# Sparse attention followed by a Mish MLP: three hand-assigned two-bank accumulators, scores in five jobs at three points of MLP2, VectorE masks placed between the normalisations

## The chip, the cores and the metric

One core of one Trainium2 chip. The metric is the device time of one execution in microseconds (us). One core alone can't be compared with another.

## The reference, cut to what matters

```python
# q, k, v: [8 batches, 8 heads, 576, 64]; heads 0-3 local, heads 4-7 strided
mask_local   = (rel >= 0) & (rel < 32)                        # rel = query - key position
mask_strided = (rel >= 0) & (key % 32 == query % 32)
attn = softmax(where(mask, q @ k.T / 8, -1e9)) @ v
x = attn.transpose(0, 2, 1, 3).reshape(4608, 512)             # 4608 tokens
h = x @ w_in                                                  # 512 -> 2048
out = (h * tanh(softplus(h))) @ w_out                         # Mish, 2048 -> 512
```

## The kernel before: the parts that matter

The 4608 tokens go through the MLP in nine blocks of 512. TensorE works on block t while the attention of a later batch is woven between its matmuls: block 0 carries batch 1, blocks 1 to 6 carry batches 2 to 7, blocks 7 and 8 carry nothing. MLP1 (x to hidden) is eight groups of eight matmuls into tiles called `psh` (in PSUM, the memory that matmuls write, eight banks of it); MLP2 (hidden to out) is sixteen steps of four matmuls into `pso`. After each MLP2 step the list below is served: `Q` computes scores and starts their exponential on ScalarE (and the mask, on the engine given), `V` multiplies masked scores by v on TensorE (the P.V below, into an output bank `po`) and normalises on VectorE, which frees that bank, `X` transposes the result into `xT`.

```python
def attn_steps(b):
    return [
        [Q("s", 0, Dv)], [], [Q("s", 1, Dv)],
        [Q("s", 2, Po), V("s", 0)],
        [Q("l", 0, Po), V("s", 1)],
        [Q("l", 1, Po), V("s", 2), V("s", 3)],
        [Q("l", 2, Po), V("s", 4)], [V("s", 5), V("s", 6)],
        [V("s", 7), V("l", 0)], [V("l", 1)], [X("s", 0), V("l", 2)],
        [X("s", 1), V("l", 3)], [X("l", 0), V("l", 4)], [V("l", 5)],
        [X("l", 1)], [],
    ]
```

So scores are entered six times a block; four of six masks are on GpSimd (`Po`), two on VectorE (`Dv`). The eight PSUM banks are split between two two-bank tiles for the MLP, one two-bank tile for scores, and two one-bank tiles for transposes and P.V outputs:

```python
ps_mm = ...tile_pool(name="psmm", bufs=2, space=PS)   # psh, pso: 2 x 2 banks
ps_s  = ...tile_pool(name="pss",  bufs=1, space=PS)   # ps: scores, 1 x 2 banks
ps_t  = ...tile_pool(name="pst",  bufs=2, space=PS)   # tr, trx, po: 2 x 1 bank
```

The prologue computes the attention of batch 0 and ends with GpSimd's own queue of work for batch 1 and 2. It is an ordered queue: what is written later waits for what is written earlier.

```python
cast_qk_loc(1, Po, Po)      # GpSimd: fp32 to bf16
cast_v(1, Po, Po)           # waits for v of batch 1 to land
load_w_out(2, 4)            # GpSimd issues: second half of w_out
load_qk_str(2)              # GpSimd issues: ks, qs of batch 2
```

The softmax here doesn't subtract the row's maximum and nothing guards it: scores larger than these inputs give would overflow.

## Time and profile before

| | before |
|---|---|
| median of 3 runs (lowest, highest) | 341.49 us (340.92, 341.49) |
| span of the profiled run | 339.5 us |
| block 0: MLP1, MLP2 | 16.45, 23.11 us |
| blocks 1 to 6: MLP1, MLP2 | 15.9 (block 4: 16.06), 19.54 us |
| blocks 7, 8: each half | 13.81 us |

The lengths of the halves are read from TensorE's timeline: from the first `psh` matmul to the first `pso`, and from there to the next first `psh`. A few matmul records are missing from a trace, so a half is now and then shown 0.2 us long and its neighbour as much short. GpSimd's queue in block 0, from the timeline (start, length, engine, line, operation, output<-input, count, and in brackets the idle time before it and what ended it):

```profile
44.98 1.89 POOL L146 CAST vs<-vs 72x2048 bf16<-72x2048 f32 x1 [15.62 <-DMA vs<-in_v_dram]
...
50.98 1.50 POOL L137 DMA_DIRECT2D w_out<-in_moe_w_out_dram  x2
...
55.41 1.29 POOL L256 TENSOR_TENSOR Ps<-Ps,consts_sb 72x576 bf16<-72x576 bf16 x1
56.64 4.83 POOL L256 TENSOR_TENSOR Pl<-Pl,consts_sb 128x768 bf16<-128x768 bf16 x3
```

The mask at 55.41 is last in the queue, behind casts and issues. TensorE stands for it before its P.V at 56.76. The cast at 44.98 could not start before v of batch 1 had landed.

### The profile page before, as it was taken

To read this page: it belongs to the slowest core of one execution; us is meant where nothing else is said; L and a number is where in the kernel's file an instruction comes from. 1 tells how busy PE (TensorE), PEld (TensorE's weight loads), DVE (VectorE), ACT (ScalarE), POOL (GpSimd) and SP (SyncE) were. 2 spreads that over 40 slices of the span, in tenths; PEclk is the share of its full clock that TensorE was granted. 3 is DMA by queue.
4 is the path that set the end of the run, shared out by engine and by line. 5 is a ranking of instruction groups with operands and counts; after the bars stand their busy time and mean duration, and the time that the engine had idled before them with its cause. 6 is when DMAs were issued, how large, how long until landed. Compare 5 with 4: busy or idle time off the path is not lost.

```text
span 339.5 us, 6425 instructions
## 1 busy us (share of the span) xinstructions
PE 313.8 (92%) x2761; PEld 171.1 (50%) x2808; DVE 114.3 (34%) x306; ACT 176.2 (52%) x194; POOL 111.0 (33%) x105
## 2 busy tenths in 40 slices
PE   2669996999999999999999999999999999999994
PEld 1554553554455545554579555544554454444441
DVE  4670345323552346134622362236323640000000
ACT  3574562556637563747464646564566537414511
POOL 4354049334681049102921094008500700000000
PEclk9999999999999999999999999999999999999999
DMA  6999958999947911595149712941010011011011
GB/s 178 217 220 205 212 95 128 215 200 284 193 110 209 188 37 64 159 198 79 63 116 202 120 62 64 229 74 60 17 51 0 2 64 62 2 62 62 0 57 68
DMA packets 49596, 39.29 MB, mean 116 GB/s; under 512 B 27168, under 2 KB 42080, under 8 KB 49568
## 3 DMA queue, kind: packets, MB, share of 16 engines
q1 hardware_dynamic: 38272, 29.88, 38.6%
q0 software_dynamic: 11152, 8.92, 16.9%
q8 instruction: 22, 0.36, 0.5%
q10 hardware_dynamic: 144, 0.08, 0.1%
q14 instruction: 6, 0.05, 0.1%
HBM read 38.34 MB, written 9.44 MB: 141 GB/s over the span
## 4 chain that ended last, share of the span: by engine, by line
PE 73%; DMA 12%; DVE 4%; POOL 3%; issue 3%; ACT 3%; SPq 1%; POOLq 0%; ACTq 0%
PE psh L368 32%; PE pso L388 28%; DMA vl<-in_v_dram 7%; DMA qs<-in_q_dram 4%; PE po L271 4%; PE tr L174 2%; PE tr L183 2%; ACT Ps L247 2%; DVE x_s L283 1%; PE ps L229 1%; DVE qTl L146 1%; PE ps L240 1%; PE trx L320 1%; PE trx L310 1%; POOL vl L146 1%
## 5 line engine op out<-in xcount | busy, mean ns | idle before, releaser
L388 PE MATMUL pso<-w_out,gT 128*128 128x512 bf16 x546 | 137.3, 379 | 1.6 <-issue 0.2
L368 PE MATMUL psh<-xT,w_in 128*128 128x512 bf16 (+1 forms) x623 | 133.1, 359 | 1.3 <-ACT gT L373 0.2
L373 ACT ACTIVATE gT<-psh 128x1024 bf16<-128x1024 f32 x72 | 73.6, 1024 | 55.7 <-PE psh L368 55.6
L368 PEld LDWEIGHTS <-w_in 128*128 128x128 bf16 x640 | 60.1, 98 | 54.6 <-issue 2.2
L388 PEld LDWEIGHTS <-gT 128*128 128x128 bf16 x576 | 49.0, 97 | 44.3
L144 ACT COPY xT<-trx 128x576 bf16<-128x576 bf16 x32 | 20.3, 639 | 44.1 <-PE trx L320 28.0
L256 POOL TENSOR_TENSOR Ps<-Ps,consts_sb 72x576 bf16<-72x576 bf16 x7 | 8.9, 1273 | 88.8 <-ACT Ps L247 88.7
L256 POOL TENSOR_TENSOR Pl<-Pl,consts_sb 128x768 bf16<-128x768 bf16 x21 | 33.8, 1638 | 1.6 <-ACT Pl L247 1.6
L395 ACT COPY osb<-pso 128x1024 f32<-128x1024 f32 x18 | 18.2, 1012 | 27.4 <-PE pso L388 27.4
L282 DVE RECIPROCAL rden<-po 72x4 f32<-72x4 f32 (+1 forms) x100 | 17.7, 177 | 35.3 <-PE po L271 35.3
L247 ACT ACTIVATE Pl<-ps 128x768 bf16<-128x768 f32 x24 | 19.5, 811 | 14.6 <-PE ps L229 14.4
L283 DVE TENSOR_TENSOR x_s<-po,rden 72x256 bf16<-72x256 f32 x56 | 23.6, 421 | 1.9
L247 ACT ACTIVATE Ps<-ps 72x864 bf16<-72x864 f32 (+1 forms) x24 | 19.1, 806 | 9.5 <-PE ps L240 9.4
L146 DVE COPY kTl<-tr 128x576 bf16<-128x576 bf16 x14 | 10.6, 758 | 30.2 <-PE tr L183 30.2
L146 POOL CAST vs<-vs 72x2048 bf16<-72x2048 f32 x7 | 13.3, 1896 | 18.3 <-DMA vs<-in_v_dram 18.3
L283 DVE TENSOR_TENSOR x_l<-po,rden 96x256 bf16<-96x256 f32 x44 | 18.5, 420 | 1.5
L256 DVE TENSOR_TENSOR Ps<-Ps,consts_sb 72x864 bf16<-72x864 bf16 (+1 forms) x17 | 10.3, 605 | 22.0 <-ACT Ps L247 22.0
L146 DVE COPY kTs<-tr 128x576 bf16<-128x576 bf16 x14 | 6.4, 458 | 30.7 <-PE tr L174 30.7
L271 PEld LDWEIGHTS <-Ps 72*128 72x128 bf16 x256 | 12.1, 102 | 8.8 <-POOL Ps L256 2.4
L271 PE MATMUL po<-vs,Ps 72*128 72x65 bf16 x224 | 14.2, 195 | 2.3 <-POOL Ps L256 2.3
L146 DVE COPY qTl<-tr 128x576 bf16<-128x576 bf16 x14 | 10.6, 756 | 14.8 <-PE tr L183 14.8
L271 PE MATMUL po<-vl,Pl 128*128 128x65 bf16 x176 | 12.9, 196 | 2.8 <-DVE rden L282 1.5
(61 smaller groups left out, 227.0 us busy)
## 6 DMA issues: line engine op xcount, KB each, us to landing
out_dram<-osb SPq DMA_DIRECT2D x18, 512.0 KB, 3.5
vl<-in_v_dram SPq DMA_DIRECT2D x7, 768.0 KB, 17.2
vs<-in_v_dram SPq DMA_DIRECT2D x8, 576.0 KB
kl<-in_k_dram SPq DMA_DIRECT2D x7, 576.0 KB
ql<-in_q_dram SPq DMA_DIRECT2D x7, 576.0 KB, 9.6
w_out<-in_moe_w_out_dram POOLq DMA_DIRECT2D x4, 512.0 KB, 12.5
ks<-in_k_dram POOLq DMA_DIRECT2D x7, 288.0 KB, 12.4
qs<-in_q_dram POOLq DMA_DIRECT2D x7, 288.0 KB, 13.8
```

What stands on the lines that cost most here:

```text
L144: nc.scalar.copy(out_, in_)
L146: eng.tensor_copy(out_, in_)
L174: nc.tensor.transpose(tr[:, PN * u:PN * u + PN], src[0:PN, h, 128 * jj:128 * jj + 128], ident[0:PN, 0:PN],)
L247: nc.scalar.activation(pt[0:n, :, 0:nw], ps[0:n, :, 0:nw], AF.Exp, scale=scale)
L256: meng.tensor_tensor(out=pm, in0=pm, in1=mk[0:n, :].unsqueeze(1).unsqueeze(1).to_broadcast([n, 2, nu, w]), op=ALU.mult,)
L271: nc.tensor.matmul(po[:, h, :], lhsT=pt[0:n, c0:c0 + 128], rhs=rhs, start=True, stop=True,)
L282: nc.vector.reciprocal(rden[0:m, :], po[0:m, :, D])
L283: nc.vector.tensor_tensor(out=dst.rearrange("p (h d) -> p h d", h=4), in0=po[0:m, :, 0:D], in1=rden[0:m, :].unsqueeze(2).to_broadcast([m, ...
L368: nc.tensor.matmul(ps[:, u, o:o + n], lhsT=w_in[:, cc, fc * 128:(fc + 1) * 128], rhs=xT[:, cc, a:a + n], start=(cc == 2), stop=(cc == 1),)
L373: nc.scalar.activation(gT[:, 2 * g:2 * g + 2, :], ps[:], AF.Mish)
L388: nc.tensor.matmul(p[:, ot % 2, :], lhsT=gT[:, fc, 128 * ot:128 * ot + 128], rhs=w_out[:, fc, :], start=(fc == 0), stop=(fc == 15),)
L395: nc.scalar.copy(osb[:], p[:])
```

## The change

Its intent: give TensorE fewer, larger visits to the scores; free the masks from GpSimd's queue and from its slower arithmetic; and let the six banks of the two-bank tiles serve whatever needs them. The diff, cut to its core:

```diff
-    ps_mm = ...tile_pool(name="psmm", bufs=2, space=PS)
-    ps_s = ...tile_pool(name="pss", bufs=1, space=PS)
+    ps_a = ...tile_pool(name="psa", bufs=1, space=PS)
+    def acc(i, name):                                  # three of these, chosen by hand
+        return ps_a.tile([128, 2, 512], F32, tag=f"acc{i}", name=name)
...                                                     # local jobs: 5, 5 and 2 units, not 4, 4, 4
-    def attn_steps(b):
+    def attn_steps(b, x, y):                           # x, y: accumulators for scores
+        if x == y:  ...                                # block 0: one accumulator, five points
         return [
+            [],
+            [Q(x, s0), Q(y, s1), M(*s0), M(*s1)],      # M: a mask, on VectorE
+            [],
+            [V("s", 0), V("s", 1)],
+            [Q(x, *sl2), Q(y, l0), V("s", 2)],         # sl2: s2 and l2 in one accumulator
+            [V("s", 3), M("s", 2), M("l", 2)],
+            [V("s", 4), M(*l0)],
+            [Q(x, l1), V("s", 5)],
+            [V("s", 6), V("l", 5), M(*l1)],
+            [V("s", 7), V("l", 0)],
+            [V("l", 1)],
+            [X("s", 0), V("l", 2)],
+            [X("s", 1), V("l", 3)],
+            [V("l", 4), X("l", 0)],
             [X("l", 1)], [],
         ]
...                                                     # mlp1 group g: accumulator g % 3
         cast_qk_loc(1, Po, Po)
-        cast_v(1, Po, Po)
-        load_w_out(2, 4)
         load_qk_str(2)                                 # now ahead of the cast of v
+        def cast_v1():                                 # called in block 0, after MLP2 step 0
+            cast(Dv, vs[1][0:PN, :, :, 0:D], vs32[0:PN])
+            Po.tensor_copy(held[:], vs[1][0:1, 3, 0, 0:4])
+            load_w_out(2, 4)
+            cast_v_loc(1, Po)
```

More of the change, by code (lines that the diff above doesn't have):

```diff
@@ L71 @@
     kTs = const.tile([128, 4 * 4 * PN + 64], BF16, name="kTs")
-    P_s = [const.tile([PN, 2, 6 * PN + 56], BF16, name=f"Ps{i}") for i in range(3)]
-    P_l = [const.tile([128, 2, 4 * WQ + 32], BF16, name=f"Pl{i}") for i in range(3)]
+    P_s = [const.tile([PN, 2, n * PN + 56], BF16, name=f"Ps{i}") for i, n in enumerate((6, 6, 4))]
+    P_l = [const.tile([128, 2, n * WQ + 32], BF16, name=f"Pl{i}") for i, n in enumerate((5, 5, 2))]
     gate = const.tile([1, 256], BF16, name="gate")
@@ L82 @@
     PS = bass.MemoryType.PSUM
-    ps_mm = ctx.enter_context(tc.tile_pool(name="psmm", bufs=2, space=PS))
-    ps_s = ctx.enter_context(tc.tile_pool(name="pss", bufs=1, space=PS))
+    ps_a = ctx.enter_context(tc.tile_pool(name="psa", bufs=1, space=PS))
     ps_t = ctx.enter_context(tc.tile_pool(name="pst", bufs=2, space=PS))
-    def tile_s(from_mm=False):
-        if from_mm:
-            return ps_mm.tile([128, 2, 512], F32, tag="mm", name="ps")
-        return ps_s.tile([128, 2, 512], F32, tag="ps", name="ps")
+    def acc(i, name):
+        return ps_a.tile([128, 2, 512], F32, tag=f"acc{i}", name=name)
     def tile_t(name):
@@ L214 @@
     S_UNITS = [(jj, h) for jj in range(4) for h in range(4)]
-    S_JOBS = [S_UNITS[0:6], S_UNITS[6:12], S_UNITS[12:16]]
-    S_AT = {u: (i, n) for i, job in enumerate(S_JOBS) for n, u in enumerate(job)}
+    L_UNITS = [(i, hp) for i in range(NW) for hp in range(2)]
+    PARTS = {
+        "s": [S_UNITS[0:6], S_UNITS[6:12], S_UNITS[12:16]],
+        "l": [L_UNITS[0:5], L_UNITS[5:10], L_UNITS[10:12]],
+    }
+    AT = {kd: {u: (i, n) for i, p in enumerate(PARTS[kd]) for n, u in enumerate(p)} for kd in "sl"}
     class Attn:
@@ L220, in __init__ @@
             self.b = b
-        def qk(self, kind, i, meng, from_mm=False):
-            ps = tile_s(from_mm)
-            if kind == "l":
-                nu, n, w, pt, mk = 4, 128, WQ, P_l[i], loc
-                for u in range(nu):
-                    hp, c0 = u // 2, WQ * (2 * i + u % 2)
-                    for e in range(2):
-                        nc.tensor.matmul(
-                            ps[:, e, WQ * u:WQ * u + WQ],
-                            lhsT=kTl[64 * e:64 * e + 64, hp, c0:c0 + 128],
-                            rhs=qTl[64 * e:64 * e + 64, hp, c0:c0 + WQ],
-                            start=True, stop=True,
-                        )
-            else:
-                nu, n, w, pt, mk = len(S_JOBS[i]), PN, PN, P_s[i], stm
-                for u, (jj, h) in enumerate(S_JOBS[i]):
-                    c0 = PN * (4 * h + jj)
-                    for e in range(2):
-                        nc.tensor.matmul(
-                            ps[:, e, PN * u:PN * u + PN],
-                            lhsT=kTs[64 * e:64 * e + 64, c0:c0 + 128],
-                            rhs=qTs[64 * e:64 * e + 64, c0:c0 + PN],
-                            start=True, stop=True,
-                        )
-            nw = nu * w
-            nc.scalar.activation(pt[0:n, :, 0:nw], ps[0:n, :, 0:nw], AF.Exp, scale=scale)
-            if meng is not None:
-                self.mask(kind, i, meng)
@@ new lines, in qk @@
+        def qk(self, parts, i_acc):
+            ps, o = acc(i_acc, "ps"), 0
+            todo = []
+            for kind, i in parts:
+                w = WQ if kind == "l" else PN
+                o0 = o
+                for x, y in PARTS[kind][i]:
+                    for e in range(2):
+                        r = slice(64 * e, 64 * e + 64)
+                        if kind == "l":
+                            lhsT, rhs = kTl[r, y, WQ * x:WQ * x + 128], qTl[r, y, WQ * x:WQ * x + WQ]
+                        else:
+                            c0 = PN * (4 * y + x)
+                            lhsT, rhs = kTs[r, c0:c0 + 128], qTs[r, c0:c0 + PN]
+                        nc.tensor.matmul(ps[:, e, o:o + w], lhsT=lhsT, rhs=rhs, start=True, stop=True)
+                    o += w
+                todo.append((kind, i, o0, o - o0))
+            for kind, i, o0, nw in todo:
+                n, pt = (128, P_l[i]) if kind == "l" else (PN, P_s[i])
+                nc.scalar.activation(pt[0:n, :, 0:nw], ps[0:n, :, o0:o0 + nw], AF.Exp, scale=scale)
@@ L251, in mask @@
         def mask(self, kind, i, meng):
-            nu, n, w, pt, mk = (
-                (4, 128, WQ, P_l[i], loc) if kind == "l" else (len(S_JOBS[i]), PN, PN, P_s[i], stm)
-            )
+            nu = len(PARTS[kind][i])
+            n, w, pt, mk = (128, WQ, P_l[i], loc) if kind == "l" else (PN, PN, P_s[i], stm)
             pm = pt[0:n, :, 0:nu * w].rearrange("p e (u c) -> p e u c", u=nu)
@@ L265, in pv_mm @@
                     n, rhs = 128, vl[self.b % 2][:, i, h, :]
-                    pt, c0 = P_l[i // 2][:, h % 2], WQ * (2 * (h // 2) + i % 2)
+                    part, u = AT["l"][i, h // 2]
+                    pt, c0 = P_l[part][:, h % 2], WQ * u
                 else:
                     n, rhs = PN, vs[self.b % 2][0:PN, h, i, :]
-                    job, u = S_AT[i // 2, h]
-                    pt, c0 = P_s[job][:, i % 2], PN * u
+                    part, u = AT["s"][i // 2, h]
+                    pt, c0 = P_s[part][:, i % 2], PN * u
                 nc.tensor.matmul(
@@ L286, in pv, with pv2 @@
             )
-        def pv2(self, kind, i, from_mm=False):
-            po = tile_s(from_mm)[:, :, 0:4 * (D + 1)].rearrange("p e (h d) -> p e h d", h=4)
+        def pv2(self, kind, i, i_acc):
+            po = acc(i_acc, "po2")[:, :, 0:4 * (D + 1)].rearrange("p e (h d) -> p e h d", h=4)
             m = WQ if kind == "l" else PN
@@ L327, in xt @@
                 )
-    def attn_steps(b):
+    def attn_steps(b, x, y):
         a = Attn(b)
-        Po, Dv = nc.gpsimd, nc.vector
-        Q = lambda kd, i, e: (lambda: a.qk(kd, i, e))
+        Q = lambda i_acc, *parts: (lambda: a.qk(parts, i_acc))
+        M = lambda kd, i: (lambda: a.mask(kd, i, nc.vector))
         V = lambda kd, i: (lambda: a.pv(kd, i))
         X = lambda kd, hf: (lambda: a.xt(kd, hf))
-        return [
-            [Q("s", 0, Dv)], [], [Q("s", 1, Dv)],
-            [Q("s", 2, Po), V("s", 0)],
-            [Q("l", 0, Po), V("s", 1)],
-            [Q("l", 1, Po), V("s", 2), V("s", 3)],
-            [Q("l", 2, Po), V("s", 4)], [V("s", 5), V("s", 6)],
-            [V("s", 7), V("l", 0)], [V("l", 1)], [X("s", 0), V("l", 2)],
-            [X("s", 1), V("l", 3)], [X("l", 0), V("l", 4)], [V("l", 5)],
+        s0, s1, sl2, l0, l1 = ("s", 0), ("s", 1), (("s", 2), ("l", 2)), ("l", 0), ("l", 1)
+        if x == y:
+            return [
+                [], [Q(x, s0)],
+                [M(*s0), Q(x, s1)],
+                [V("s", 0)],
+                [V("s", 1), M(*s1), Q(x, *sl2)],
+                [V("s", 2)],
+                [V("s", 3), M("s", 2), M("l", 2), Q(x, l0)],
+                [V("s", 4)],
+                [V("s", 5), M(*l0), Q(x, l1)],
+                [V("s", 6), V("l", 5)],
+                [V("s", 7), V("l", 0), M(*l1)],
+                [X("s", 0), V("l", 1)],
+                [X("s", 1), V("l", 2)],
+                [V("l", 3), V("l", 4)],
+                [X("l", 0), X("l", 1)], [],
+            ]
+        return [
+            [],
[12 more added lines that the diff above has]
+            [V("l", 4), X("l", 0)],
             [X("l", 1)], [],
@@ L353, in segs, with mlp1 @@
         return r
-    def mlp1(t):
+    def mlp1(t, accs):
         gT = g_pool.tile([128, 16, 512], BF16, tag="gT", name="gT")
@@ L361, in group @@
             if g not in held:
-                held[g] = ps_mm.tile([128, 2, 512], F32, tag="mm", name="psh")
+                held[g] = acc(accs[g % 3], "psh")
             ps = held[g]
@@ L378, in mlp1, with mlp2 @@
         return gT, [lambda g=g: group(g) for g in range(8)]
-    def mlp2(t, gT, fc_major=False):
+    def mlp2(t, gT, accs, fc_major=False):
         po = {}
@@ L384, in group @@
             if ot // 2 not in po:
-                po[ot // 2] = ps_mm.tile([128, 2, 512], F32, tag="mm", name="pso")
+                po[ot // 2] = acc(accs[ot // 2], "pso")
             p = po[ot // 2]
@@ L447 @@
         for i in range(3):
-            a.qk("s", i, None, i > 0)
+            a.qk([("s", i)], i)
         a.mask("s", 0, Dv)
@@ L460 @@
             t_step_loc0(kl0, kTl[:, hp, 32:32 + S], hp, Sc)
-        a.pv2("s", 0)
+        a.pv2("s", 0, 0)
         a.mask("s", 2, Dv)
-        a.pv2("s", 2, True)
+        a.pv2("s", 2, 1)
         for hp in range(2):
             t_step_loc0(ql0, qTl[:, hp, :], hp, Sc)
-        a.qk("l", 0, None, True)
-        a.pv2("s", 4)
-        a.qk("l", 1, None, True)
+        a.qk([("l", 0)], 2)
+        a.pv2("s", 4, 0)
+        a.qk([("l", 1)], 1)
         a.mask("l", 0, Dv)
-        a.pv2("s", 6)
+        a.pv2("s", 6, 0)
         cast_v_loc(0, Sc, 3, 6)
-        a.qk("l", 2, None, True)
+        a.qk([("l", 2)], 2)
         a.mask("l", 1, Dv)
@@ L477 @@
         load_v(1)
-        gT, g1 = mlp1(0)
+        accs = (2, 1, 0)
+        gT, g1 = mlp1(0, accs)
         a.xt("s", 0)
@@ L481 @@
         Sc.preload_act_table(AF.Mish)
-        a.pv2("l", 0, True)
+        a.pv2("l", 0, 1)
         a.mask("l", 2, Dv)
-        a.pv2("l", 2)
+        a.pv2("l", 2, 0)
         a.pv("l", 4)
@@ L499 @@
         for t in range(NBLK):
+            x, y, z = accs
             if t > 0:
-                gT, g1 = mlp1(t)
-            ts = t_steps(t + 1) if t + 1 < B else []
-            at = attn_steps(t + 1) if t + 1 < B else []
+                gT, g1 = mlp1(t, accs)
+            ts, at = [], []
             if t == 0:
+                ts, at = t_steps(1), attn_steps(1, y, y)
                 at[8].append(load_next)
-                at[0] = ts[2:4] + at[0] + [lambda: load_qk_str(3)]
+                at[0] = ts[2:4] + [cast_v1, lambda: load_qk_str(3)]
+                out_accs, accs = (z, x), (y, z, x)
+            else:
+                if t + 1 < B:
+                    ts, at = t_steps(t + 1), attn_steps(t + 1, x, y)
+                out_accs, accs = (z, y), (z, x, y)
             for i, g in enumerate(g1):
@@ L515 @@
                 load_qk_str(t + 3)
-            for i, g in enumerate(mlp2(t, gT, fc_major=(t == 0))):
+            for i, g in enumerate(mlp2(t, gT, out_accs, fc_major=(t == 0))):
                 g()
```

## The prediction

> **What bounds the kernel now.** I read the page first: busy shares, then the chain that ended last, then stretches by windows, then the timeline of one repeating block, and the timeline of the first block apart.
>
> ```profile
> PE 313.8 (92%) x2761; PEld 171.1 (50%) x2808; DVE 114.3 (34%) x306; ACT 176.2 (52%) x194; POOL 111.0 (33%) x105
> PE psh L368 32%; PE pso L388 28%; DMA vl<-in_v_dram 7%; DMA qs<-in_q_dram 4%; PE po L271 4%; PE tr L174 2%; PE tr L183 2%; ACT Ps L247 2%; DVE x_s L283 1%; PE ps L229 1%; DVE qTl L146 1%; PE ps L240 1%; PE trx L320 1%; PE trx L310 1%; POOL vl L146 1%
> ```
>
> TensorE sets the time: psh and pso, the two MLP layers, are 60% of the chain, and no other engine is over 52% busy. So only what lengthens or interrupts TensorE's stream counts. There are nine token blocks: block 0 carries the attention of batch 1, blocks 1 to 6 that of batches 2 to 7, blocks 7 and 8 none. One repeating block, MLP1 then MLP2:
>
> ```profile
> 172.60:188.70 16.10, 16.10 (x185) 14.57 (x184) 4.10 (x7) 9.54 (x11) 1.49 (x2) 1.00 0.98 190
> 188.70:208.25 19.55, 19.02 (x205) 10.04 (x207) 10.00 (x31) 10.68 (x13) 12.54 (x10) 1.00 0.26 61
> ```
>
> Columns: stretch, us, busy of PE, PEld, DVE, ACT, POOL, clock, DMA share, GB/s. Both halves hold 64 full matmuls' worth. Eight of these and the start of the next kind are 1.73 us apart (212.22 to 213.95), 0.2165 each, so 13.86 us a half. MLP1 adds eight groups of transposes at about 0.25: 15.9, no loss. MLP2's 19.55 has 5.7 us of small work, and the timeline shows that part of this is not work:
>
> ```profile
> 189.97 1.90 PE L388 MATMUL pso<-w_out,gT 128*128 128x512 bf16 x8
> 191.93 0.37 PE L240 MATMUL ps<-qTs,kTs 64*128 64x72 bf16 x12
> 192.23 1.04 PE L388 MATMUL pso<-w_out,gT 128*128 128x512 bf16 x4
> ...
> 195.01 1.03 PE L388 MATMUL pso<-w_out,gT 128*128 128x512 bf16 x4
> 195.97 0.34 PE L229 MATMUL ps<-qTl,kTl 64*128 64x96 bf16 x8
> 196.25 0.42 PE L271 MATMUL po<-vs,Ps 72*128 72x65 bf16 x8
> ...
> 200.39 0.29 PE L271 MATMUL po<-vl,Pl 128*128 128x65 bf16 x4 [0.25 <-DVE rden L282]
> ```
>
> Starts matter, not durations. Four matmuls from 195.01 end their issue at 195.88, yet the scores start at 195.97: 0.09 lost on entering. Scores take 0.28 for eight (195.97 to 196.25) and 0.30 for twelve of 72 columns (191.93 to 192.23); eight of 72 take 0.24. The slope is 15 ns a matmul, half of 72 columns at the full matmuls' 512 / 0.2165 = 2.4 a ns (the two row halves run together), and 0.12 stays over. **Each entry into the scores thus costs about 0.10 + 0.12 = 0.22 us**, whatever its size. At 191.93 the wait is 0.23 instead of 0.10, and the chain says why: the second scores job needs the one scores buffer that the first exponential has just left.
>
> ```profile
> 190.99 0.90 ACT Ps L247
> 191.88 0.04 issue
> 191.93 0.37 PE ps L240 x12
> ```
>
> Block 0 has a loss of its own. GpSimd casts v, issues six loads and only then masks; TensorE stands:
>
> ```profile
> 54.20 0.29 PE L271 MATMUL po<-vs,Ps 72*128 72x65 bf16 x4
> 56.76 0.29 PE L271 MATMUL po<-vs,Ps 72*128 72x65 bf16 x4 [2.27 <-POOL Ps L256]
> ```
>
> **What the Trainium skill says.** "TensorEngine Tiling (Array Packing)", Key Properties: changing the tiling mode, not merely the tile, drains TensorE. The scores use 64-row tiles, everything around them 128-row ones; the 0.22 us above agrees in kind (the page has no figure). "GPSIMD Engine Reference", Engine selection: two-input elementwise work is about twice as slow there as on VectorE. Here the factor is larger: the 72x576 mask took 1.273 us on GpSimd, 0.446 on VectorE. Its Key points say the two share SBUF interfaces when VectorE reads two SBUF inputs; the trace agrees once: the mask at 46.57 took 0.76 instead of 0.60 with GpSimd's v cast running. "Perfetto Trace Analysis", Optimization Strategy: a gap that repeats on the saturated engine can mean too few buffers for the next tile; the wait at 191.93 is one.
>
> **The change, part by part.** Instruction counts on TensorE and ScalarE's exponentials (six a block) stay. VectorE gains the four masks a block that GpSimd did.
>
> *Entries.* Six a block (after MLP2 steps 0, 2, 3, 4, 5, 6) become three (after 1, 4, 7): two jobs share a point because each has its own accumulator. 3 x 0.22 = 0.66 us off.
>
> *Scores buffer.* Two waits for an exponential, 0.13 (191.93) and 0.07 (193.27), go: 0.20 off. The scores start one step later, so the table load (189.69 to 190.97, ScalarE) is nearly done when they end: the first exponential starts at about the same time.
>
> *Masks on VectorE.* By width from 0.446 (576 elements), 0.545 (768) and 0.614 (864), 0.55 ns an element: 0.65 for each 960-wide local job, 0.34 for the 384-wide one, 0.45 for s2; some 2.1 us a block more. VectorE goes from 10.0 to 12.1 us of MLP2's 19.5, but it is in order, and P.V needs its output bank back (two banks) after a normalisation, 0.56 us each back to back. I walked the queue step by step with the measured delays (P.V start to reciprocal 0.34, normalisation end to next P.V 0.13). TensorE would wait 0.1 to 0.2 at step 8, 0.3 to 0.4 at step 9 and 0.2 at step 10: V(l,5), V(l,0) and V(l,1), behind mask l0 and mask l1. Sum about 0.65. The stall before the P.V at 200.39, counted from the issue of the four at 199.85 (0.54 less 0.11), is 0.43 and goes. Net 0.2 lost.
>
> A block: 19.55 - 0.66 - 0.20 + 0.2 = 18.9, **0.6 us less; six blocks, 3.7 us.**
>
> *Three accumulators in MLP1.* No steady loss to win: eight groups ran without a gap. In block 0's MLP1 one wait of 0.25 for the activation goes; the local mask before it is narrower. 0.3 us, earlier.
>
> *Block 0.* MLP2 took 23.1 us (43.1 to 66.2) against 19.55 + 0.5 for two more transposes: 3 us of loss, of which 2.27 + 0.30 are GpSimd's masks and 0.48 a wait for qTs. All three go, and v's cast is 1.23 on VectorE instead of 1.89. But two loads (ks, qs of batch 2) now stand ahead of the cast in GpSimd's queue, so they start at about 30 us instead of 52. They will share the DMA engines with v of batch 1, issued at 37.3 to 38. The engines ran full until about 46, and v (vs) landed at about 44.6. Shared, I put it at 45 to 47 (two loads of 288 KB at the 200 GB/s seen there are 2.9 us of all engines). VectorE then stands before the first mask until 46.3 to 48.1, and TensorE up to 1.1 us at the first P.V. The walk from there, with 0.2 to 0.5 at four later P.V and transposes, ends MLP2 at 63.4 to 64.5: 1.7 to 2.8 us less, **with the 0.3 (partly the same time) 2.1 in the middle.**
>
> Sum: 341.49 - 3.7 - 2.1 = **335.7 us**, 1.7% less. Blocks 7 and 8 are untouched.
>
> **Rivals.**
> 1. *VectorE becomes the local bound:* its masks block the normalisations, and P.V waits take back all the entries gave. For it: the chain already passes through normalisations (200.39), and three of the four new masks stand between them. Against: 12.1 of 19.5 us, and no P.V of the old kernel waited over 0.5 us in steady blocks. With 0.6 more a block: 339.3.
> 2. *Block 0 gives nothing:* v lands late behind the advanced loads, or the second half of w_out, issued after the cast at about 47 to 49 and needed at 53 to 54 (5.7 us from issue to landing before), stalls step 8. For it: DMA is 90% busy or more from 8.5 to 42 us. Against: the old kernel's own stall of 2.6 us leaves room. Alone: 337.8.
> 3. *The entry cost grows with the job,* so that merging saves only waits: the 15 ns slope for 8 and 12 speaks against. Then about 339.
> 4. *It saves more:* if the waits I walked do not occur (masks before data are needed), a block gains 1.2 us: 331.5 to 332. For it: the order of the masks looks placed to avoid them. Against: two P.V banks are unchanged.
> 5. *A hidden win:* GpSimd's casts no longer sit behind its masks. They were never waited for in steady blocks, so nothing.
>
> **Range and chances.** Steady blocks 0.6 +- 0.2 times six, block 0 2.1 +- 1: 334 to 337.5 holds most; I take 333.5 to 337.6. Faster by over 2% needs below 334.7, one microsecond under my figure: 0.3. Slower needs rival 1 and 2 together and much more: 0.01.
>
> **What would show each step.** Scores in three places a block, 24, 22 and 10 matmuls, with one gap of about 0.1 ahead of each and 0.12 over after: right if MLP2's half measures 18.7 to 19.1 and MLP1's stays 15.9 to 16.1. No TensorE wait on the exponentials; P.V waits on normalisations at steps 8 to 10, under 0.5 each. VectorE about 12 us in that half, GpSimd only casts and loads. In block 0 no wait for GpSimd's masks, a wait of up to 1.1 us at the first P.V for the mask that follows the v cast, and MLP2 of 20.5 to 21.5 us. Wrong if a P.V wait over 1 us repeats in every block, if step 8 of block 0 waits for w_out, or if the merged scores take longer than 15 to 20 ns a matmul.

## The result, and the profile after

| | before | after |
|---|---|---|
| median of the runs made together | 341.36 us (340.92 to 341.49, 4 runs) | 335.9 us (335.66 to 336.18, 4 runs) |
| ratio, 95% interval | | 0.984 [0.983, 0.986] |
| span of the profiled run | 339.5 us | 334.4 us |
| block 0: MLP1, MLP2, end | 16.45, 23.11, at 66.22 us | 16.82, 23.00, at 66.17 us |
| blocks 1 to 6: MLP2 | 19.54 us | 18.73 to 18.75 us |

The gain is real and under 2%. The total is 0.2 us from the prediction, but the table shows that two errors cancelled, which is luck: the repeating blocks gave 0.80 us each instead of 0.6, and block 0, of which 2.1 us were expected, gave 0.05.

The page after, busy shares and the chain that ended last; more of the chain is now the two MLP layers (67% where it was 60%), and VectorE has gained the 12 us that the masks and one cast of v cost it:

```profile
PE 312.5 (93%) x2808; PEld 170.8 (51%) x2808; DVE 126.1 (38%) x335; ACT 173.3 (52%) x194; POOL 68.3 (20%) x77
PE pso L409 34%; PE psh L389 33%; DMA qs<-in_q_dram 5%; DMA vl<-in_v_dram 4%; PE po L266 4%; DMA vs<-in_v_dram 3%; PE ps L239 3%; PE tr L172 2%; PE tr L181 2%; DMA w_out<-in_moe_w_out_dram 2%; PE trx L305 1%; PE trx L315 1%; DVE x_l L278 1%
```

`DMA vs` and `DMA w_out` are new in this chain. First the windows of the same repeating block as in the prediction, MLP1 and MLP2 (stretch, us, busy of PE, PEld, DVE, ACT, POOL, clock, DMA share, GB/s):

```profile
170.10:186.10 16.00, 16.00 (x184) 14.52 (x183) 4.11 (x7) 9.47 (x10) 6.20 (x5) 1.00 0.98 205
186.10:204.85 18.75, 18.51 (x209) 9.96 (x207) 11.87 (x35) 10.28 (x13) 2.34 (x3) 1.00 0.19 51
```

MLP1 is as it was. In MLP2 VectorE is busy 11.87 us of 18.75 (10.00 before). The timeline of TensorE in this MLP2, its scores and the one P.V that waits:

```profile
186.15 1.89 PE L409 MATMUL pso<-w_out,gT 128*128 128x512 bf16 x8
187.97 0.56 PE L239 MATMUL ps<-qTs,kTs 64*128 64x72 bf16 x24
188.47 1.90 PE L409 MATMUL pso<-w_out,gT 128*128 128x512 bf16 x8
...
191.41 0.30 PE L239 MATMUL ps<-qTs,kTs 64*128 64x72 bf16 x8
191.55 0.46 PE L239 MATMUL ps<-qTl,kTl 64*128 64x96 bf16 x14
...
195.02 0.39 PE L239 MATMUL ps<-qTl,kTl 64*128 64x96 bf16 x10
...
197.45 0.29 PE L266 MATMUL po<-vs,Ps 72*128 72x65 bf16 x4
197.98 0.29 PE L266 MATMUL po<-vl,Pl 128*128 128x65 bf16 x4 [0.24 <-DVE x_l L278]
```

Three entries, not six. Eight full matmuls from 186.15 end their issue at 187.88 (8 x 0.2165), the scores start at 187.97: 0.09 lost, as before, and no wait for an exponential on top. The 24 take 0.50 (to 188.47): 24 x 15 ns = 0.36 and 0.14 over. The P.V at 197.98 should start 0.12 after the one at 197.45 and starts 0.53 after it, so it cost about 0.4 (the bracket counts from a modelled end and shows less).

Then block 0, TensorE and VectorE:

```profile
50.44 0.30 PE L266 MATMUL po<-vs,Ps 72*128 72x65 bf16 x4 [2.23 <-DVE Ps L250]
...
56.06 1.02 PE L409 MATMUL pso<-w_out,gT 128*128 128x512 bf16 x4 [0.46 <-DMA w_out<-in_moe_w_out_dram]
```

```profile
48.65 1.23 DVE L144 CAST vs<-vs 72x2048 bf16<-72x2048 f32 x1 [3.32 <-DMA vs<-in_v_dram]
49.79 0.60 DVE L250 TENSOR_TENSOR Ps<-Ps,consts_sb 72x864 bf16<-72x864 bf16 x1
```

GpSimd's masks and their wait of 2.27 us are gone. In their place TensorE waits 2.23 us for a mask that stands on VectorE behind the cast of v, and the cast waits for v to land, 3.7 us later than in the kernel before (48.65 against 44.98). Step 8 then waits for w_out, whose issue now hangs on that cast.

### The profile page after: what moved, and what is told of

Its sections match the earlier page's. It is cut to its first block, busy times and chain, and to the rows that moved or that the text cites. A ratio compares the mean times of both kernels' runs of the same rounds, so it can differ in the third digit from the quotient of the medians.

```text
span 334.4 us, 6451 instructions
## 1 busy us (share of the span) xinstructions
PE 312.5 (93%) x2808; PEld 170.8 (51%) x2808; DVE 126.1 (38%) x335; ACT 173.3 (52%) x194; POOL 68.3 (20%) x77
## 4 chain that ended last, share of the span: by engine, by line
PE 79%; DMA 14%; DVE 3%; POOL 1%; SPq 1%; issue 1%; ACT 0%; ACTq 0%; POOLq 0%
PE pso L409 34%; PE psh L389 33%; DMA qs<-in_q_dram 5%; DMA vl<-in_v_dram 4%; PE po L266 4%; DMA vs<-in_v_dram 3%; PE ps L239 3%; PE tr L172 2%; PE tr L181 2%; DMA w_out<-in_moe_w_out_dram 2%; PE trx L305 1%; PE trx L315 1%; DVE x_l L278 1%; DVE x_s L278 1%; DVE rden L277 1%
## 5 line engine op out<-in xcount | busy, mean ns | idle before, releaser
L409 PE MATMUL pso<-w_out,gT 128*128 128x512 bf16 x576 | 140.6, 379 | 0.5 <-DMA w_out<-in_moe_w_out_dram 0.5
L389 PE MATMUL psh<-xT,w_in 128*128 128x512 bf16 (+1 forms) x640 | 134.7, 360 | 0.0
L409 PEld LDWEIGHTS <-gT 128*128 128x128 bf16 x576 | 49.6, 97 | 45.9 <-issue 0.6
L266 PEld LDWEIGHTS <-Ps 72*128 72x128 bf16 x256 | 14.4, 101 | 13.4 <-DVE Ps L250 2.7
L244 ACT ACTIVATE Pl<-ps 128x960 bf16<-128x960 f32 (+1 forms) x24 | 18.7, 806 | 4.2 <-PE ps L239 4.1
L266 PE MATMUL po<-vs,Ps 72*128 72x65 bf16 x256 | 17.5, 200 | 2.7 <-DVE Ps L250 2.2
L250 DVE TENSOR_TENSOR Ps<-Ps,consts_sb 72x864 bf16<-72x864 bf16 (+1 forms) x24 | 13.8, 573 | 15.9 <-ACT Ps L244 15.9
L144 POOL CAST vl<-vl 128x768 bf16<-128x768 f32 x15 | 13.2, 903 | 23.7 <-DMA vl<-in_v_dram 23.7
L144 POOL CAST kl<-kl 96x1536 bf16<-96x1536 f32 x7 | 10.3, 1472 | 32.7 <-DMA kl<-in_k_dram 32.7
L266 PE MATMUL po<-vl,Pl 128*128 128x65 bf16 x192 | 13.9, 201 | 2.3 <-DVE x_l L278 1.4
L96 POOL DMA_DIRECT2D ks<-in_k_dram x7 | 5.1, 729 | 47.6 <-PE tr L172 47.6
```

The costliest lines, as they stand in the source:

```text
L144: eng.tensor_copy(out_, in_)
L244: nc.scalar.activation(pt[0:n, :, 0:nw], ps[0:n, :, o0:o0 + nw], AF.Exp, scale=scale)
L250: meng.tensor_tensor(out=pm, in0=pm, in1=mk[0:n, :].unsqueeze(1).unsqueeze(1).to_broadcast([n, 2, nu, w]), op=ALU.mult,)
L266: nc.tensor.matmul(po[:, h, :], lhsT=pt[0:n, c0:c0 + 128], rhs=rhs, start=True, stop=True,)
L389: nc.tensor.matmul(ps[:, u, o:o + n], lhsT=w_in[:, cc, fc * 128:(fc + 1) * 128], rhs=xT[:, cc, a:a + n], start=(cc == 2), stop=(cc == 1),)
L409: nc.tensor.matmul(p[:, ot % 2, :], lhsT=gT[:, fc, 128 * ot:128 * ot + 128], rhs=w_out[:, fc, :], start=(fc == 0), stop=(fc == 15),)
```

## The experiments

"Step" is one of MLP2's sixteen, counted from 0. All runs gave a correct result. The kernel before was run beside them: median 339.93 us with the first four, 339.80 with the next four, 340.14 with the last three. Ratios are to it.

| run | median us (runs) | ratio, 95% | MLP2, repeating blocks | block 0: MLP2, end |
|---|---|---|---|---|
| the change, again | 335.26 (5) | 0.986 [0.982, 0.990] | 18.73 | 20.86, 64.72 |
| loads behind the cast | 334.43 (4) | 0.983 [0.978, 0.988] | 18.74 (block 1: 19.09) | 19.98, 65.17 |
| five entries | 338.69 | 0.996 [0.991, 1.001] | 19.16 (three blocks; others collide) | 22.66, 65.97 |
| one accumulator | 340.15 | 0.999 [0.995, 1.004] | 19.49 (block 1: 19.88) | 22.73, 65.88 |
| masks back on GpSimd | 335.62 | 0.986 [0.981, 0.991] | 18.69 | 23.17, 66.04 |
| loads behind, cast held | 334.38 (4) | 0.982 [0.978, 0.986] | 18.74 (block 1: 19.80) | 20.23, 63.47 |
| the same, masks on GpSimd | 333.74 | 0.981 [0.977, 0.984] | 18.69 | 20.14, 64.14 |
| the same, one P.V moved | 330.97 (5) | 0.972 [0.968, 0.976] | 18.29 | 20.13, 64.27 |
| that one again | 330.92 (4) | 0.972 [0.967, 0.976] | 18.29 | 20.42, 63.54 |
| that one, two accumulators in MLP1 | 332.07 (4) | 0.975 [0.971, 0.979] | 18.29 (18.07 with a record missing) | 20.14, 64.86 |
| masks straight after their scores | 354.88 (4) | 1.043 [1.038, 1.047] | 21.35 (block 1: 24.33) | 20.98, 65.45 |

### 1. The change once more, as a base on the same chip

> The changed kernel as it is, as the measure for its neighbours on this chip (the kernel before took 341.4 us on the first chip and 339.9 on the second). Expected: 0.982 to 0.987 of the kernel before; a repeating block's MLP2 18.7 to 18.8 us, block 0's 22 to 23.2. If theory H (a mask on VectorE that starts while GpSimd casts is held until that cast ends) holds, masks over 0.7 us appear where a cast covers their start, and nowhere else.

Measured: 335.26 us, repeating blocks 18.73 as before. Block 0 is different in this run: v's last packet landed at 45.9 us (packet records of the trace) instead of 47.3, and TensorE came later to MLP2 (43.86 instead of 43.17), so that the first P.V did not wait. Theory H holds: the two masks over 0.7 us (0.88 at 88.29, 1.15 at 119.23) both began under a cast of GpSimd. Of the six profiled runs that have the loads in this place, four end block 0 at 65.9 to 66.2 and two at 64.7 and 65.5. The loss in block 0 is thus usual, not certain, and a figure for block 0 from one trace is worth about 1 us.

One cause of that spread has nothing to do with the change. The first matmuls of MLP1(0) start 0.427 us apart and later ones 0.216; the slow ones were 4 to 10 in a run, before and after alike (4 in before, 7 in after, 9 here). The Trainium skill, "TensorE: Matmul & The Clock Gate", Part 1, says that a cold TensorE runs at half rate until a free-running activity window of about 3.4 us was busy, so that the number of slow matmuls varies from run to run of one kernel. The trace agrees: its clock records grant the full clock from 28.46 us on in before and from 29.31 in after, for 91 and 89 times 3.413 us; the slow matmuls end at 28.4 and 29.3. (The clock column of the windows doesn't show it.)

### 2. The two loads back behind the cast of v

```diff
         cast_qk_loc(1, Po, Po)
-        load_qk_str(2)
...
-                at[0] = ts[2:4] + [cast_v1, lambda: load_qk_str(3)]
+                at[0] = ts[2:4] + [cast_v1, lambda: load_qk_str(2), lambda: load_qk_str(3)]
```

> The changed kernel, with only the two loads of batch 2's ks and qs put back behind the cast of v (and behind w_out) in GpSimd's queue. Theory A (these loads, advanced, share the DMA engines with v of batch 1 and made it land 3.7 us later, 48.6 instead of 45.0): v's cast starts at 45 to 45.5 us, the first P.V of block 0 no longer waits 2.2 us for its mask, the wait of 0.46 for w_out goes too, and block 0's MLP2 falls from 23.0 to 20.5 to 21.2 us; time 333.6 to 334.3 us. Rival B (v is late because its cast and the mask now stand in one in-order queue on VectorE, or because v is issued late): MLP2 of block 0 stays at 22.5 to 23 us, time 335.5 to 336.2.

Measured: MLP2(0) 19.98 us instead of 23.00, 0.5 below the range expected of the theory that the advanced loads make v late. TensorE and VectorE of block 0:

```profile
49.20 1.04 PE L409 MATMUL pso<-w_out,gT 128*128 128x512 bf16 x4
50.07 0.28 PE L266 MATMUL po<-vs,Ps 72*128 72x65 bf16 x4
```

```profile
47.26 1.22 DVE L144 CAST vs<-vs 72x2048 bf16<-72x2048 f32 x1
48.87 0.60 DVE L250 TENSOR_TENSOR Ps<-Ps,consts_sb 72x864 bf16<-72x864 bf16 x1 [0.40 <-ACT Ps L244]
```

The cast has no wait in front of it, the P.V follows its step at once (0.87 after it, four times 0.2165), and v's last packet landed at 43.5 us. The packet records of all thirteen profiled kernels, with v issued at 36.6 to 37.9 us in every one:

| v of batch 1, 288 packets | loads ahead (6 kernels) | loads behind (7, with before) |
|---|---|---|
| half of them started by | 42.7 to 43.9 us | 40.9 to 42.3 us |
| last one landed | 45.9 to 47.5 us | 43.5 to 44.6 us |
| mean time of a packet | 155 to 172 ns | 122 to 133 ns |

v is not only begun later: its packets take longer and the delay grows while it runs. From 37.3 us to v's last packet, GpSimd's queue moved 989 to 1149 packets of 1 KB beside it with the loads ahead, and 406 to 646 with the loads behind. So the order of two lines in GpSimd's queue is the cause, and the rival that something else delays v falls.

The 3 us of MLP2(0) did not all reach the end: the ratio, 0.983, is only 0.001 to 0.003 under the two of the changed kernel (0.4 to 1 us), which is inside its interval: by the total alone this run isn't shown to be faster than the change. In the profiled run the prologue lost 2 us. The same mask in the changed kernel and here, with GpSimd's cast that ran beside the second one:

```profile
23.56 0.34 DVE L250 TENSOR_TENSOR Pl<-Pl,consts_sb 128x384 bf16<-128x384 bf16 x1
```

```profile
23.82 1.82 DVE L250 TENSOR_TENSOR Pl<-Pl,consts_sb 128x384 bf16<-128x384 bf16 x1
```

```profile
23.93 1.50 POOL L144 CAST kl<-kl 96x1536 bf16<-96x1536 f32 x1
```

The mask, 0.34 us alone, lasted until 0.2 us after the cast had ended, and a P.V stood 2.11 us for it. The Trainium skill, "SBUF — State Buffer", Who interferes with whom, calls the port pair that VectorE shares with GpSimd an exclusive lock. This agrees. In the thirteen traces 27 of VectorE's 476 masks took longer than they do alone. Each met a cast of GpSimd and ended 0.22 to 0.51 us after it, which is the mask's own time less 0.12 to 0.15, whether much or little of the cast was left: such a mask is not slowed, it stands until the cast is through. It goes the other way too: in 23 meetings the cast is the one that stood (19 of them are casts of 0.83 us alone that ended 0.69 after the mask). Whether cast and mask meet is chance here: GpSimd reached this cast at 23.9 us in some runs and at 26.6 in others, by how long an issue before it had to wait.

### 3. Two more entries into the scores

```diff
-            [Q(x, s0), Q(y, s1), M(*s0), M(*s1)],
-            [],
+            [Q(x, s0), M(*s0)],
+            [Q(y, s1), M(*s1)],
...
-            [Q(x, *sl2), Q(y, l0), V("s", 2)],
-            [V("s", 3), M("s", 2), M("l", 2)],
+            [Q(x, *sl2), V("s", 2)],
+            [Q(y, l0), V("s", 3), M("s", 2), M("l", 2)],
```

> The changed kernel with the scores at five points of MLP2 instead of three in blocks 1 to 6 (one job a point, the same two accumulators, the same masks). Theory C (each entry into the 64-row scores costs 0.22 us whatever its size): MLP2 of a repeating block goes from 18.74 to 19.1 to 19.3 us, time 338.2 to 339.2. Rival D (the entries are free where no wait is in them, the gain came from the accumulators alone): 18.7 to 18.8 a block, time 335.7 to 336.2.

Measured: 19.15 to 19.16 us in the undisturbed blocks, 0.42 more for two more entries: 0.21 each, the prediction's 0.22. Jobs, accumulators, masks and P.V are the same in both, so the entry cost is shown directly. In three blocks masks met GpSimd casts (block 1: 1.26 and 1.43 us instead of 0.60 and 0.45) and took more; the median is the worse for it.

### 4. One accumulator for the scores in all blocks

```diff
-                    ts, at = t_steps(t + 1), attn_steps(t + 1, x, y)
+                    ts, at = t_steps(t + 1), attn_steps(t + 1, x, x)
```

> The changed kernel with the schedule of its block 0 in all blocks: one accumulator for the scores, five points. Theory C (0.22 us an entry, plus a wait of TensorE for the exponential that leaves the one accumulator): two entries more are 0.44, the wait for the first exponential 0.1 to 0.3, so MLP2 of a repeating block 19.2 to 19.6 us and time 338.8 to 340.5. If the accumulators were the whole gain (D), the same figure, but the five-entry kernel with two accumulators would then stay at 336. If neither: 336.

Measured: 340.15 us, 19.49 a block, 0.75 more than the change. Two entries more are 0.42 of it; the second scores job again starts 0.23 instead of 0.10 after its step, as in the kernel before; what makes the remaining 0.2 was not separated, since this list also places the P.V otherwise. What it settles: with one accumulator, this list and every mask on VectorE, the change gains nothing (0.999). The second accumulator, with the merging that it allows, is where the gain lies, apart from that 0.2 for the list.

### 5. The masks back on GpSimd in blocks 1 to 6

```diff
-        M = lambda kd, i: (lambda: a.mask(kd, i, nc.vector))
+        M = lambda kd, i: (lambda: a.mask(kd, i, nc.gpsimd if x != y
+                           and (kd, i) not in (("s", 0), ("s", 1)) else nc.vector))
```

> The changed kernel with the masks of s2, l2, l0 and l1 on GpSimd again in blocks 1 to 6, called at the same places; s0 and s1 and all of block 0 stay on VectorE. Theory E (the 0.5 us that TensorE still waits at steps 8 to 10 come from the round trip of the two P.V banks, not from the masks on VectorE, and GpSimd's masks are in time): MLP2 of a repeating block 18.6 to 18.9 us, time 335.0 to 336.8. Rival F (the masks on VectorE were part of the gain): 19.0 or more a block, time over 337.5. Rival G (the masks on VectorE cost what I put to them, 0.2 or more a block): 18.5 or less, time under 334.8.

Measured: 18.69 to 18.70 us a block, 0.05 below the change. The wait of step 9, at 197.98 in the changed kernel, is still there:

```profile
197.18 0.29 PE L266 MATMUL po<-vs,Ps 72*128 72x65 bf16 x4
197.71 0.29 PE L266 MATMUL po<-vl,Pl 128*128 128x65 bf16 x4 [0.24 <-DVE rden L277]
```

The second P.V starts 0.53 after the first, as before, though VectorE now has no mask between its normalisations there. So that wait is not the masks': two steps with two P.V each follow one another, and there are two output banks (theory E). Moving the four masks to VectorE was therefore worth nothing in the repeating blocks, and cost as little: this part of the change is bookkeeping there.

### 6. Loads behind, and the cast held back

```diff
+        Po.tensor_copy(held[:], x_l[0:1, 5, 0:4])      # a wait for the last local normalisation
         cast_qk_loc(1, Po, Po)
```
(with the edit of experiment 2)

> The loads of ks and qs put back behind the v cast, and GpSimd's cast of kl held until the last normalisation of batch 0. Theory H (the first attempt lost 1.5 to 2 us before the first matmul because GpSimd's kl cast began with the last mask on VectorE and that mask took 1.82 us instead of 0.34): the mask is back at 0.34, the first MLP1 matmul at 26.3 to 26.9 us instead of 28.5, MLP2 of block 0 stays at 20 to 20.5, and the time is 2.4 to 3.2 us under the changed kernel's of the same rounds, with less spread than the 1.8 us of the first attempt. If the loss had another cause: the first matmul at 28 again in some runs and a spread over 1.5 us.

Measured: 334.38 us, 0.9 under the change run beside it, where 2.4 to 3.2 were expected: a miss. What the hold was to mend came as expected: the mask took 0.34, the first matmul of MLP1 is at 26.93, the runs are within 0.65 us. Two reasons are in the traces. The base itself had one of its good block 0s (64.72; here 63.47). And the collision moved: the prologue is clean, but block 1 took 19.80 us. VectorE and GpSimd in block 1:

```profile
83.34 1.61 DVE L250 TENSOR_TENSOR Ps<-Ps,consts_sb 72x864 bf16<-72x864 bf16 x1 [0.17 <-ACT Ps L244]
...
88.61 1.85 DVE L250 TENSOR_TENSOR Pl<-Pl,consts_sb 128x960 bf16<-128x960 bf16 x1
```

```profile
82.88 1.61 POOL L144 CAST ql<-ql 96x1536 bf16<-96x1536 f32 x1 [1.25 <-DMA ql<-in_q_dram]
88.07 1.89 POOL L144 CAST vs<-vs 72x2048 bf16<-72x2048 f32 x1 [3.57 <-DMA vs<-in_v_dram]
```

Both masks began while a cast ran and ended about 0.5 us after it (alone: 0.60 and 0.65 us).

### 7. The same with the late masks of blocks 1 to 6 on GpSimd

(the edits of experiments 5 and 6 together)

> The same with the masks of s2, l2, l0 and l1 on GpSimd in blocks 1 to 6, so that its casts come after them and no cast meets a mask of VectorE. From the earlier pair, 0.05 us a block and the collisions: 0.2 to 0.8 us under the held kernel. If VectorE's masks were a benefit, slower.

Measured: 333.74 us, 0.64 under experiment 6, all six blocks at 18.68 to 18.70, no mask on VectorE longer than 0.61 us in them (one of 0.69 in block 0). Work on GpSimd's own queue can't meet GpSimd's casts.

### 8. One P.V a step earlier

```diff
-            [Q(x, l1), V("s", 5)],
-            [V("s", 6), V("l", 5), M(*l1)],
+            [Q(x, l1), V("s", 5), V("l", 5)],
+            [V("s", 6), M(*l1)],
```
(on top of experiment 7)

> The same with the P.V of the last local window one step earlier (step 7 instead of 8), so that the two steps with two P.V each are no longer neighbours. Theory E (what TensorE still loses at steps 8 to 10 is the round trip of the two P.V banks): the waits of about 0.45 us a block fall to 0.1, MLP2 of a repeating block 18.3 to 18.4 us, time 1.8 to 2.4 us under the kernel without the move. If the banks are not the limit: no change, or a new wait at step 8.

Measured: 330.97 us, 2.8 under experiment 7, and 18.29 us in each block: 0.40 less. The steps around it on TensorE, without any wait:

```profile
192.07 0.29 PE L266 MATMUL po<-vs,Ps 72*128 72x65 bf16 x4
192.20 0.29 PE L266 MATMUL po<-vl,Pl 128*128 128x65 bf16 x4
...
194.19 0.29 PE L266 MATMUL po<-vs,Ps 72*128 72x65 bf16 x4
194.31 0.29 PE L266 MATMUL po<-vl,Pl 128*128 128x65 bf16 x4
```

The P.V at 194.31 is the one that stood 0.4 us at 197.98 in the changed kernel; here it follows its neighbour by 0.12. V l5 uses a mask that was ready long before (l2), so it can be served while ScalarE works on l1; one step later it and the next pair of P.V need the two output banks faster than VectorE can empty them. The version repeats: 330.92 us.

> The combined version again (loads behind the v cast, GpSimd's cast held, masks of blocks 1 to 6 on GpSimd, P.V l5 one step earlier), as the base of the run before it on the same chip, and to see whether its gain repeats: 330.3 to 332 us, MLP2 of repeating blocks 18.29 within 0.03.

It beats both kernels: 2.8% under the one before by the ratio, and 1.3% under the change by the medians (330.97 to 335.26).

### 9. The same with two accumulators in MLP1

```diff
-                held[g] = acc(accs[g % 3], "psh")
+                held[g] = acc(accs[g % 2], "psh")
```

> The combined version that ran at 330.97 us, with MLP1 rotating over two accumulators instead of three, everything else left. Theory L: the third accumulator in MLP1 is worth nothing in repeating blocks (eight groups ran without a gap on two) and at most one wait of 0.2 to 0.5 us in block 0: MLP1 of repeating blocks 15.9, 331.0 to 331.8 us. Rival M: with three the activation of a group may lag behind the scores' exponentials at the change of halves, and the third buffer hides it: then MLP1 of each repeating block is 0.2 to 0.5 us longer, 332.5 to 335 us.

Measured: MLP1 of the repeating blocks unchanged. In block 0 the third group starts 0.628 us after the matmul before it instead of 0.216: one wait of 0.41 us, on the first Mish. The runs, 330.88 to 332.36 us, are spread too widely to weigh it (this trace also had ten slow first matmuls against six), so the value of the third accumulator in MLP1 rests on that one gap: 0.4 us once, nothing in steady blocks.

### 10. Each mask straight after its scores

```diff
-            [Q(x, *sl2), Q(y, l0), V("s", 2)],
-            [V("s", 3), M("s", 2), M("l", 2)],
-            [V("s", 4), M(*l0)],
-            [Q(x, l1), V("s", 5)],
-            [V("s", 6), V("l", 5), M(*l1)],
+            [Q(x, *sl2), Q(y, l0), M("s", 2), M("l", 2), M(*l0), V("s", 2)],
+            [V("s", 3)],
+            [V("s", 4)],
+            [Q(x, l1), M(*l1), V("s", 5)],
+            [V("s", 6), V("l", 5)],
```

> The changed kernel, but in blocks 1 to 6 each VectorE mask is called straight after its scores (s2, l2, l0 ahead of P.V s2; l1 ahead of P.V s5) instead of between later normalisations. Theory J: the placing matters, since VectorE works in order and then stands before a mask until its exponential is done, with normalisations behind it that P.V needs: MLP2 of a repeating block 19.2 to 19.7 us against 18.73 to 18.75, with TensorE waits at P.V s4 and later, 338.5 to 341.5 us in all. Rival K: the placing is a nicety, two P.V banks cover it: 18.7 to 18.9 and 335.2 to 336.3.

Measured: 354.88 us, 4% over the kernel before, and 21.35 us a block (one at 21.73; block 1 24.33). The theory that placing matters holds, but its size was far off: 2.6 us a block, not 0.5 to 1.0. ScalarE, VectorE and TensorE of one block, in this order:

```profile
243.97 1.01 ACT L416 COPY osb<-pso 128x1024 f32<-128x1024 f32 x1 [2.53 <-issue]
244.88 0.98 ACT L244 ACTIVATE Pl<-ps 128x960 bf16<-128x960 f32 x1
```

```profile
245.89 0.66 DVE L250 TENSOR_TENSOR Pl<-Pl,consts_sb 128x960 bf16<-128x960 bf16 x1 [2.13 <-ACT Pl L244]
246.46 0.17 DVE L277 RECIPROCAL rden<-po 72x4 f32<-72x4 f32 x1
```

```profile
244.14 0.29 PE L266 MATMUL po<-vs,Ps 72*128 72x65 bf16 x4
...
245.14 0.28 PE L266 MATMUL po<-vs,Ps 72*128 72x65 bf16 x4
247.23 0.29 PE L266 MATMUL po<-vl,Pl 128*128 128x65 bf16 x4 [1.81 <-DVE rden L277]
```

The scores of l1 started at 243.82 and took 0.3, but ScalarE first copied an output tile, so the exponential began at 244.88 and ended about 245.9. VectorE stood 2.13 us in front of the mask although two P.V results (244.14, 245.14) waited behind it to be normalised; they held both output banks, and the third P.V stood. My expectation had left out the output copy that stands ahead of the exponential. That is about 0.7 us of the loss. Another P.V of this block, at 242.73, had stood before in the same way, behind a normalisation that stood behind the mask of l0. Counted by starts, the two waits are 1.08 and 1.97 us; less the 0.44 us of waits that a block of the change has, this is the whole 2.61.

Block 1 is a case of its own. A mask there met a cast (1.76 us at 88.96), a P.V stood 2.02 us until 91.33, and from 92.92 to 99.74 us the clock records grant TensorE half its clock (the windows 92:96 and 96:100 show 0.61 and 0.53, with full matmuls 0.43 apart). Its 24.33 us is thus collision and clock together. In the other blocks of this run, with waits up to 1.8 us, the clock stayed full, so the 21.35 isn't touched.

## Why the prediction was right in total, and where its steps were wrong

**Entries: right.** Three fewer entries at 0.22 us were to give 0.66 a block. The timeline after shows the same 0.09 ahead of an entry and 0.12 to 0.14 left over for 24 matmuls as for 8 or 12; experiment 3 gives 0.21 for one. The third rival, that the cost grows with the job, falls.

**Scores buffer: right.** No score waits for an exponential after the change; experiment 4 brings one such wait back, at its old 0.23.

**P.V stalls: right that step 9 stalls, wrong in what makes it stall, and the term too large.** The walk gave 0.1 to 0.2 at step 8, 0.3 to 0.4 at step 9 and 0.2 at step 10, about 0.65, "behind mask l0 and mask l1", so +0.2 net. Counted by starts, the trace has nothing at step 8, 0.41 at step 9 (197.98) and 0.03 at step 10: 0.44, so +0.01 net. The two waits that the masks were to make hardly came, and the one that came is not theirs: experiment 5 keeps it without those masks, experiment 8 removes it (0.40 us a block) by parting the two pairs of P.V. With 0.44 the sum is 0.66 + 0.20 - 0.01 = 0.85, and 0.80 was measured; six blocks give 4.8, not 3.7. (The prediction's own terms make 0.66 a block and 4.0 for six; it rounded down.) The fourth rival (no stalls, 1.2 us a block) is about what that version reaches: 19.54 - 18.29 = 1.25. The first rival, VectorE as the bound, does not describe the change (11.87 of 18.75 us busy), but experiment 10 shows how near it lies: not by the amount of work, by its order.

**Masks on VectorE: right that they cost little.** Experiment 5 shows also that they bring nothing in the repeating blocks, and experiments 2, 6 and 7 that they may now meet GpSimd's casts. The prediction had seen one such meeting (0.76 instead of 0.60) and left it out of the sum; a full one makes a mask 1.0 to 1.5 us longer, and up to 1.1 us of a block (experiment 6, block 1).

**MLP1 with three accumulators: right.** 0.3 us predicted in block 0; the gap ahead of the third group is 0.628 in before, 0.216 after, so 0.41, and experiment 9 brings it back. It can't be seen in the length of the half, since the changed kernel's profiled run had three more slow first matmuls (7 against 4, 0.21 us each).

**Block 0: wrong.** This is the step that failed: "Shared, I put it at 45 to 47", from which came "TensorE up to 1.1 us at the first P.V", MLP2(0) of 20.5 to 21.5 us and 2.1 us of gain. The mechanism was named: the loads that now stand ahead of the cast share the DMA engines with v. Its size was not: v's last packet came at 47.3 in the profiled run, the cast started at 48.65, and TensorE stood 2.23 us plus 0.46 at step 8. Both are what the second rival said, "block 0 gives nothing", and experiment 2 proves it by its opposite: loads behind the cast, MLP2(0) of 19.98. With the prologue clean as well (experiment 6), block 0 ends at 63.47, where the prediction had put 63.4 to 64.5. The estimate in the same sentence, 2.9 us for the two loads at the full rate, was near the delay of v's last packet (47.33 - 43.87 = 3.5 us). Taking it whole instead of 0.4 to 2.4 of it, and adding the 1.1 to 1.3 us from the last packet to the start of the cast in both traces, would have given the cast at 47.9 and a stall of some 1.5 us; the range of 45 to 47 had assumed a share that the packets don't show.

So the sum came out by 1.1 us more from the repeating blocks against 2.05 us less from block 0. That leaves 0.75 us: the profiled spans fell by 5.1 us (4.8, 0.05, a wait of 0.13 for qs in block 1's MLP1, and some 0.1 after block 6), the medians by 5.5 and 0.1 of the base is another median (341.36 for 341.49). What is left is within the spread of single runs.

## What to carry to other kernels

Merging visits to a differently tiled matmul pays by the visit (0.21 us here), and it needs an extra accumulator more than it needs faster masks. On an engine that works in order, put a job where its input is already there: the same masks on the same engine cost 2.6 us a block when they stood one or two places too early, and a P.V one step earlier won 0.4. Moving work to another engine also moves what it can meet: masks on VectorE stood for GpSimd's casts, up to 1.1 us of a block, and masks on GpSimd did not. When an edit moves a load forward in one queue, ask what else is in flight then: two lines that nobody waited for took back the whole gain of the first block.

## What the Trainium skill lacked or had wrong

- "TensorEngine Tiling (Array Packing)", Key Properties: it says that a change of tiling mode drains TensorE, without a figure. Going into 64-row scores between 128-row matmuls and back cost 0.21 to 0.22 us a visit here, for 8, 12, 22 and 24 matmuls alike.
- "GPSIMD Engine Reference", Engine selection: about twice as slow as VectorE for two-input work. The 72x576 bf16 mask took 1.273 us against 0.446, a factor of 2.9.
- "SBUF — State Buffer", Who interferes with whom: the lock is as told. The page has no figure for when the held operation ends: here it ended 0.12 to 0.15 us less than its own time after the holder did (27 masks). Which of the two came first can't be read from close starts, since starts on GpSimd are rough in a trace: a mask whose record starts 0.10 us ahead of the cast's stood for all of it (23.82, 23.93), and four that start 0.04 to 0.06 ahead did not.
- "TensorE: Matmul & The Clock Gate", Part 1: it names 6, 11 and 14 slow matmuls for one kernel and says that the number varies, as it does here (4 to 10). What it doesn't say is what that hides: about 1.3 us between the extremes, more than the 0.4 us that one of these experiments was after.
- "DMA: Bandwidth & Descriptors", Issuing engines are not separate DMA queues: it says that the queues of different engines run on the same 16 DMA engines and interleave. The runs agree, and give what the page has no figure for: two loads of 288 KB in GpSimd's queue made one of 576 KB in SyncE's queue land 1.3 to 4 us later, with packets of 155 to 172 ns instead of 122 to 133.
